# Attention output turned by a stored copy and turning transfers instead of on TensorE, with x's third piece in two and k's first part issued later

## The chip, the cores and the metric

The kernel runs on one core of a Trainium2 chip. The metric is device time in microseconds (us) for one execution, as the median of several runs. A core has five engines that run side by side and meet through semaphores: TensorE (PE; its weight loads are listed apart as PEld), VectorE (DVE), ScalarE (ACT), GpSimd (POOL) and SyncE (SP). SP computes nothing here; it issues transfers, and its instructions are taken strictly in order, as are those of every engine.

## The reference

Two branches on the same x (= A_q, 2048 tokens by 640 channels, bf16) are mixed by a gate per token.

```python
x = A_q
g = _sigmoid((x * gate_w).sum(-1, keepdims=True))
a = _A_ref(x, A_k, A_v, A_shift_k, A_ssm_k, A_ssm_D)
b = _B_ref(x, B_wqkv, B_wo)
return g * a + (1 - g) * b
```

Branch A takes a causal four-tap convolution of k per channel, multiplies it by v, convolves the product along the whole sequence with a kernel of 2048 taps per channel (by a transform of length 4096, plus `ssm_D` times the input) and multiplies by q. Branch B is attention with 32 heads of 20 channels, in which each token sees the 8 tokens at distances 0, 2, ..., 14 behind it, followed by the output projection:

```python
qkv = (x @ wqkv).reshape(B, S, 3, H, Dh)          # H = 32, Dh = 20
idx = pos[:, None] - off[None, :]                 # off = 0, 2, ..., 14
logits = jnp.einsum("bhsd,bhswd->bhsw", q, kg) * scale
attn = _softmax(jnp.where(mask, logits, -1e9), axis=-1)
o = jnp.einsum("bhsw,bhswd->bhsd", attn, vg)
return o.reshape(B, S, D) @ wo
```

## The kernel before

**Layout.** Even and odd tokens are two separate sequences ("parities") of 1024, since the attention's distances are even. Each is cut into 9 blocks of 114 queries that see 121 keys (`BQ`, `BK`), 18 blocks in all; the last block of a parity has 112 queries. x is wanted with channels on partitions (`xT`, five tiles of 128 channels): it is turned on its way in by turning transfers (`load_x`, line 291), for parity 0 in pieces of 256, 256 and 512 rows (`x00`, `x01`, `x02`), for parity 1 in two of 512 (`x10`, `x12`).

**Order.** Every step is a generator that yields one request per instruction group. Which generator goes next, and whether ScalarE or VectorE empties a PSUM buffer, was settled beforehand: the string `ORDER` has one letter per request, `ENGINES` one letter per free choice of engine, and `Plan.run` (line 159) only replays them. Each engine therefore has a fixed list. The PSUM is four slots of two banks, handed out in turn in that same order, so an instruction on TensorE also waits for the evacuation that last used its slot. The costs in the requests play no part in the replay.

**The steps, in rough order of time.**

- `heads` (line 374): first loads and constants. On POOL's queue: the gate's weights, the taps (`wraw`), k's first part (rows 50 to 63 of each group of 64, four transfers, line 399), and then the mask rows of the second key and query buffers (`masks`, line 369: a copy for keys, one for queries).
- `vproj` (line 470): value projection, 9 units of two blocks for each half of the heads; a unit is ten matmuls, evacuated to `VW`.
- `qkproj` (line 512): q and k projection, five channel tiles, three units of ten matmuls for q and for k, evacuated to `stg`; `fragger` (line 546) moves the heads' rows from there to 32-row slots of the key and query buffers, by transfers on POOL's queue (`kb`, `qb`). Eight sets of four heads share three buffers.
- `conv` (line 445): the four-tap convolution, on VectorE, from the last rows down, 7 instructions on 11 rows each; it needs k's parts as they land.
- `score_gen` (line 583), `pv_gen` (line 608): for each head set ten groups of scores, exponentials on ScalarE, two groups of attention times values, and on VectorE the normalisation into `oS` (tokens of a block on partitions, 18 blocks by 640 channels).
- `transform` (line 682): the forward transform in two stages (`s1_unit`, 10 units; `s2_unit`, 11 units) for the kernel h and the input u, each in two halves of the channels: "h units" and "u units" below. Stage 1 of u reads `vin` as weights. h's taps come in 16 slices on SP's queue (line 333); POOL adds `ssm_D` to h (line 711) when its half is there; G (the second stage's matrix) comes in four pieces into the buffer that the convolution leaves.
- `swaps` (line 743): per half, eight transfers of 320 KB that write the transform of h with its partition halves exchanged (`Hw`). From the fourth on each is preceded by a `link` (line 277), a tiny transfer that waits for the one three before.
- `op_tr` (line 780): the attention output turned on TensorE, 18 matmuls against an identity for each of five channel tiles, each tile copied from PSUM to `oT` by one instruction. `oT` lies where h's taps lay.
- `products` (line 695): 22 products on VectorE per half; they need the half's `Hw` whole.
- `outproj` (line 796): 16 groups of 40 matmuls from `oT` and `wo`, evacuated with the factor 1 - g to `bl`.
- `inverse1` (line 763), `final` (line 847), `load_q`, `gate_q`, `stores`: the inverse transform in two stages, q gated by g, the mix, and the stores of the result.

The order in which the generators are numbered by `ORDER`'s letters is that of lines 885 to 890.

Of the kernel before, what the change touches and what calls it, by code (L numbers as in the profile page):

```python
# [17 lines left out]
S = 2048  # L18
D = 640
# [32 lines left out]
def _np_bf16(a):  # L52
    return np.asarray(a, dtype=np.float32).astype(ml_dtypes.bfloat16)
# [35 lines left out]
def attn_consts():  # L89
# [19 lines left out]
    return dict(mm=_np_bf16(mm.reshape(128, BK + BQ)), ident=_np_bf16(np.eye(128)))  # L109
# [4 lines left out]
aaaafawaxaaaaaaaxxwwwwaxwgaaxxjjwfwxwfffxxwfwjxxfjjxffffffffffjacjjjccjjcjaxffcwaawwjwacacccccxacfcwwawbjajffaajcjcbaddjdcdajdfbdddaajajddcc  # L114
djjccddajadcddedcbddbadcaccfxxxffcfecjfacedxbjaefcbbcddjdddjadjdfdjfcddcjddajcdddedaddacfjedjddfddadddjeccacccdadjcaddjdafcdaecdfdecddjcecdc
cdacdjdbaffjddaaacjfedjdddcaejffaadjddfdjdfddbdedjaadddbbejdefccchaacaacjcjckcccaaejbcmcchdkcdaddjachcdjdddjdddjdjddkdadhjekadddjaddikcaekja
ddmdjadjdlcAcccAdceddAedddAbAdAAddecdddcccdAdeccdcddAdAdcAeadcedAddAAdddcAaadAdAAdAdlednddddaeaadAaAadelddkedddlAdAdAAdAdAAAlddledldldAdemmB
ddBAABBABeeBBBlABoBCABBBBBBBABlCABClABqAqBkCACqAqAqACCDDCDCCCCCCClCCqlllCDqCDqlDCpDqCqqpBBBBBBBBBBBBDDDDBpBBBBBpBBBCBlDCCDCCCCDCDDDDDDCDClpC
CCCDpppppppDpDpyDyDplyyDrrryrDCyryDDyDpypryCDryCCrDyyyyCryCDrDDrCyCyDDDrDyDrDppyppprypppyprrrprpDslEsErEEsEsEEEEEEEEEzzzzzzzzzzzzzzzzzzzzzzE
EEEEsFsEFFtsFssEFssFFtFFtFtsFFFFFFFsFFssFrtsrtsusFusuuuuuuuuuuuuuuuuuuuuurrruruuuuuuusuuturururrrvutruuuuuvurvvruvvuvvvvvvvvvvvvvvvvvvvvvv  # L120
"""
ENGINES = """
ADDAADAAAAAAAAAAAAAADAADDDDAADADADDDDAADDAADDDDDDDDDDDDDADDDADDADAADADAADADADAADADAADADADADADADADADADAADADADADADADADAADADAAAAADAAAAAADAAAAAA
AAAAAAAAAAAAAADADDADADDDAAAADDDDAAADAASDASSSASSSSSSSSSSSSSSSSSSASASAS
# [53 lines left out]
def kernel(  # L178
# [21 lines left out]
    def raw(ap, off, dims):  # L200
        return bass.AP(tensor=ap.tensor, offset=ap.offset + off, ap=dims)
# [6 lines left out]

    p0 = ctx.enter_context(tc.tile_pool(name="p0", bufs=1))
# [7 lines left out]
    ident = p0.tile([128, 128], BF, name="ident")  # L217
# [151 lines left out]
    def masks(copier, e):  # L369
        nc.gpsimd.memset(ksets[e][:, KW:], 0.0)  # L370
        copier(ksets[e][:, 0:KW].rearrange("p (b k) -> p b k", k=BK), mm[:, 0:BK].unsqueeze(1).to_broadcast([128, NB, BK]))
        copier(qsets[e][:].rearrange("p (b k) -> p b k", k=BQ), mm[:, BK:BK + BQ].unsqueeze(1).to_broadcast([128, NB, BQ]))

    def heads():
# [22 lines left out]
        a, b = KR[0]  # L397
        for q in range(4):
            nc.gpsimd.dma_start(kin[32 * q:32 * q + 32, 3 + a:3 + b, :], raw(k2, a * D + CH[q], [[64 * D, 32], [D, b - a], [1, QC]]))
        masks(nc.gpsimd.tensor_copy, 1)  # L400
# [5 lines left out]
        for q in range(4):  # L406
            at(f"k{q}0", 15500.0)
# [3 lines left out]
    def late():  # L411
# [16 lines left out]
    XP = {"x00": (0, 0, 256), "x01": (0, 256, 512), "x02": (0, 512, 1024), "x10": (1, 0, 512), "x12": (1, 512, 1024)}  # L428
# [179 lines left out]
    def pv_gen():  # L608
        n = 0
        for t in range(NT):  # L610
            for gis, b0, na in PARTS:
# [21 lines left out]
                for a in range(na):  # L633
                    dst = oS[0:BQ, b0 + 6 * a:b0 + 6 * a + 6, 80 * t:80 * t + 80].rearrange("p b (h d) -> p b h d", h=4)
                    nc.vector.tensor_tensor(dst, Ov[:, a, :, 0:DH].rearrange("p (b h) d -> p b h d", h=4),
                                            rv[:, a].rearrange("p (b h) -> p b h", h=4).unsqueeze(3).to_broadcast([BQ, 6, 4, DH]), ALU.mult)
        mark("oS", r)
# [141 lines left out]

# [142 lines left out]
```

## Time and profile before

| | us |
|---|---|
| median of 3 runs | 232.32 |
| lowest, highest | 231.50, 232.58 |
| the profiled execution's own time | 232.02 |
| its span, first to last instruction | 229.9 |

| engine | busy, us | share of the span | instructions |
|---|---|---|---|
| TensorE, matmuls | 209.2 | 91% | 3802 |
| VectorE | 189.2 | 82% | 259 |
| ScalarE | 165.3 | 72% | 215 |
| POOL | 63.6 | 28% | 144 |

The mean clock granted to TensorE is 0.924 of full speed. 34.92 MB are moved in 74,742 packets, 58,276 of which are under 512 bytes.

How the lines below are read. The chain of waits gives, in order of time, start, length and what the chain was on: an engine with its line, or a transfer with its two tensors; "SPq" is SP issuing a transfer. A line of the timeline or of the group table reads: line of the kernel, engine, operation, output<-input by the program's names, shapes, count; the group table goes on with busy time, mean ns of one, and the idle time ahead of them with what ended it. Names such as `sc`, `pj`, `psv`, `s`, `i`, `op`, `tr` are PSUM tiles of the steps above. `SX` holds h's first half after the convolution, `Hs` the second, `UC` holds u.

### The profile page before, as it was taken

Reading aid. Unit: us, or ns where it says so; the run is one execution under the profiler, and the core shown is the slowest. Engines: PE = TensorE matmul, PEld = TensorE weight load, DVE = VectorE, ACT = ScalarE, POOL = GpSimd, SP = SyncE. Lnnn points to the kernel's source line nnn. Section 1 sums busy time; section 2 is a strip of 40 time slices with the busy share of each in tenths; the row PEclk is TensorE's granted clock in tenths of the full one; section 3 lists DMA queues with packets and bytes.
Section 4 is the critical chain, followed back from the end, with each engine's and each line's share of the span. In section 5 each row is a group of like instructions: output and inputs, shape, how many; then the busy total and the mean of one; then the engine's idle time right before and its main releaser. Section 6 shows DMA issues by size and latency. Waiting matters only on the chain.

```text
span 229.9 us, 8777 instructions
## 1 busy us (share of the span) xinstructions
PE 209.2 (91%) x3802; PEld 168.2 (73%) x3802; DVE 189.2 (82%) x259; ACT 165.3 (72%) x215; POOL 63.6 (28%) x144
## 2 busy tenths in 40 slices
PE   6859999999899999999898998999899999999940
PEld 2647978857656766566676788898798899998930
DVE  4353999779868989977997679999999998979990
ACT  2012535378498888587888879979999999788960
POOL 8891005945734754745500000000000000000000
PEclk9997999999999999999855557999999999999996
DMA  7999856869999999797797661096887955921872
GB/s 171 205 232 232 169 173 142 171 117 170 145 158 174 150 156 156 117 139 125 139 139 215 182 204 41 3 222 157 174 189 161 227 98 117 199 35 25 196 183 66
DMA packets 74742, 34.92 MB, mean 152 GB/s; under 512 B 58276, under 2 KB 71152, under 8 KB 74704
## 3 DMA queue, kind: packets, MB, share of 16 engines
q1 hardware_dynamic: 68896, 26.93, 61.3%
q0 software_dynamic: 4080, 6.41, 13.4%
q10 hardware_dynamic: 1728, 1.02, 1.7%
q8 instruction: 29, 0.48, 1.0%
q14 instruction: 9, 0.07, 0.1%
HBM read 18.43 MB, written 2.62 MB: 92 GB/s over the span
## 4 chain that ended last, share of the span: by engine, by line
PE 55%; DVE 18%; DMA 10%; POOL 5%; ACT 4%; issue 4%; SPq 2%; DVEq 0%; POOLq 0%; ACTq 0%
PE pj L527 13%; PE i L772 8%; PE psv L478 8%; PE op L810 6%; PE s L672 6%; PE sc L595 6%; DMA xT<-in_A_q_dram 5%; DVE Hs L207 4%; ACT ETall L602 4%; PE s L656 4%; PE O L623 4%; DMA kb<-stg 3%; DVE SX L873 3%; DVE SX L870 3%; DMA Dz<-in_A_ssm_D_dram 2%
## 5 line engine op out<-in xcount | busy, mean ns | idle before, releaser
L602 ACT ACTIVATE ETall<-sc 121x912 bf16<-121x912 f32 (+1 forms) x80 | 63.8, 858 | 10.5 <-PE sc L595 9.9
L527 PE MATMUL pj<-xT,Wqk 128*128 128x342 bf16 (+1 forms) x300 | 48.8, 312 | 0.3 <-DVE stg L207 0.3
L527 PEld LDWEIGHTS <-Wqk 128*128 128x128 bf16 x300 | 27.9, 98 | 15.0 <-issue 0.2
L205 ACT CAST UC<-s 128x960 bf16<-128x960 f32 (+2 forms) x32 | 29.4, 980 | 1.8 <-PE s L656 1.2
L478 PE MATMUL psv<-KX,xT 128*121 128x320 bf16 x180 | 27.1, 310 | 3.9 <-DMA xT<-in_A_q_dram 2.7
L478 PEld LDWEIGHTS <-xT 128*121 128x121 bf16 x180 | 24.8, 139 | 6.0 <-DMA xT<-in_A_q_dram 3.0
L572 POOL DMA_DIRECT2D qb<-stg x36 | 18.1, 505 | 35.6 <-ACT stg L205 21.8
L595 PE MATMUL sc<-qb,kb 31*128 31x114 bf16 x576 | 24.2, 232 | 2.3 <-ACT ETall L602 0.6
L436 DVE TENSOR_TENSOR KX<-KX 128x1760 bf16<-128x1760 bf16 (+1 forms) x24 | 24.6, 1042 | 0.4
L810 PE MATMUL op<-wo,oT 128*32 128x320 bf16 x640 | 24.0, 303 | 0.3 <-ACT SX L866 0.3
L205 ACT CAST VW<-psv 121x640 bf16<-121x640 f32 x13 | 8.9, 696 | 20.9 <-PE psv L478 20.9
L595 PEld LDWEIGHTS <-kb 31*128 31x128 bf16 x576 | 14.4, 101 | 12.3 <-issue 8.9
L672 PEld LDWEIGHTS <-SX 64*128 64x128 bf16 x512 | 20.5, 100 | 3.5 <-issue 2.8
L810 PEld LDWEIGHTS <-oT 128*32 128x32 bf16 x640 | 21.2, 140 | 1.4 <-issue 0.2
L205 ACT CAST stg<-pj 128x684 bf16<-128x684 f32 (+1 forms) x14 | 10.4, 742 | 16.4 <-PE pj L527 10.0
L572 POOL DMA_DIRECT2D kb<-stg x36 | 18.1, 507 | 11.6 <-DVE stg L207 5.6
L207 DVE CAST stg<-pj 128x726 bf16<-128x726 f32 (+1 forms) x16 | 14.3, 896 | 7.9 <-PE pj L527 4.7
L207 DVE CAST SX<-s 128x1024 bf16<-128x1024 f32 (+1 forms) x15 | 17.7, 1195 | 2.9 <-PE s L672 2.0
L443 DVE TENSOR_TENSOR KX<-KX 128x1760 bf16<-128x1760 bf16 (+1 forms) x18 | 18.8, 1043 | 0.4
L623 PEld LDWEIGHTS <-ETall 121*128 121x128 bf16 x576 | 16.4, 98 | 2.3 <-issue 1.2
L772 PE MATMUL i<-F,Hw 128*128 128x128 bf16 x160 | 18.0, 219 | 0.0
L772 PEld LDWEIGHTS <-Hw 128*128 128x128 bf16 x160 | 17.9, 114 | 0.0
(76 smaller groups left out, 350.7 us busy)
## 6 DMA issues: line engine op xcount, KB each, us to landing
vin<-in_A_v_dram SPq DMA_DIRECT2D x8, 320.0 KB
h_lin<-in_A_ssm_k_dram SPq DMA_DIRECT2D x16, 160.0 KB
Hw<-SX SPq DMA_DIRECT2D x8, 320.0 KB
Hw<-Hs SPq DMA_DIRECT2D x8, 320.0 KB
SX<-in_A_q_dram SPq DMA_DIRECT2D x16, 160.0 KB
kb<-stg POOLq DMA_DIRECT2D x28, 85.1 KB, 4.2
qb<-stg POOLq DMA_DIRECT2D x28, 80.2 KB, 4.3
SX<-cf_G SPq DMA_DIRECT2D x4, 512.0 KB
```

The costliest lines, as they stand in the source:

```text
L205: nc.scalar.copy(dst, src)
L207: nc.vector.tensor_copy(dst, src)
L436: eng.tensor_tensor(d, kin[:, n + 3 - j:n + 3 - j + m, :], w.to_broadcast([128, m, QC]), ALU.mult)
L478: nc.tensor.matmul(ps[0:BK, i, 0:320], lhsT=xT[:, dt, s0:s0 + BK], rhs=Wv[:, dt, 320 * hf:320 * hf + 320], start=(dt == 0), stop=(dt == ND ...
L527: nc.tensor.matmul(ps[:, i, 0:n], lhsT=Wqk[:, dt, w, 128 * ft:128 * ft + 128], rhs=xT[:, dt, s0:s0 + n], start=(dt == 0), stop=(dt == NDT ...
L572: nc.gpsimd.dma_start(dst[r0:r0 + rows, 0:wd], stg[fa - f0:fb - f0, 0:wd])
L595: nc.tensor.matmul(sc[:, hh, BQ * bb:BQ * bb + BQ], lhsT=kb[r:r + DH + NF, BK * b:BK * b + 128], rhs=qb[r:r + DH + NF, BQ * b:BQ * b + BQ] ...
L602: nc.scalar.activation(ETall[0:BK, e, :, 0:BQ * nb], sc[0:BK, :, 0:BQ * nb], ACT.Exp, scale=SCALE)
L623: nc.tensor.matmul(O[:, (b - b0) // 6, c0:c0 + 21], lhsT=ETall[0:BK, e, hh, BQ * bb:BQ * bb + 128], rhs=VW[0:BK, b, 4 * t + h4, :], start= ...
L672: nc.tensor.matmul(ps[:, c, 160 * jj:160 * jj + 160], lhsT=st["G"][rows, j0 + jj, rr, :], rhs=Am[rows, rr].rearrange("p o (q j) l -> p j ( ...
L772: nc.tensor.matmul(d, lhsT=st[(key, P)][:, c, o + il // 4, :, il % 4], rhs=M[:, k, :], start=(k == 0), stop=(k == 1), skip_group_check=True)
L810: nc.tensor.matmul(op[c:c + 32, tt, 0:320], lhsT=oT[:, ft, h, 32 * e:32 * e + 32, a], rhs=wo[:, ft, 320 * w:320 * w + 320], start=(ft == 0 ...
```

## The change

The turning on TensorE goes. In its place a generator `keep_o` stores the attention output to a DRAM buffer `o_d` (two parities, 1024 tokens, 640 channels) in three parts of the channels, as the head sets are done (sets 0 to 3, 4 and 5, 6 and 7): four transfers per part on SP's queue, two for the first 112 rows of all blocks and two for the last two rows of the first eight blocks. `op_tr` then reads it back by four turning transfers of 512 tokens each, also on SP's queue, into an `oT` with another order of its columns; the output projection takes its weights from there at a step of 32 columns. The identity and its load go. x's third piece becomes two of 256 rows (`x02`, `x03`). k's first part is issued behind the key mask's copy on POOL instead of ahead of it. `ORDER` and `ENGINES` are new strings.

```diff
-    return dict(mm=_np_bf16(mm.reshape(128, BK + BQ)), ident=_np_bf16(np.eye(128)))
+    return dict(mm=_np_bf16(mm.reshape(128, BK + BQ)))
...
     def loads():
-        yield from load_x("x00", 0, 0, 256, 1400.0, 4550.0)
-        yield from load_x("x01", 0, 256, 256, 2800.0, 3400.0)
-        yield from load_x("x02", 0, 512, 512, 4300.0, 3100.0)
+        yield from load_x("x00", 0, 0, 256, 1400.0, 5100.0)
+        yield from load_x("x01", 0, 256, 256, 2800.0, 2700.0)
+        yield from load_x("x02", 0, 512, 256, 2800.0, 2300.0)
+        yield from load_x("x03", 0, 768, 256, 2800.0, 1900.0)
...
-    def masks(copier, e):
+    def masks(copier, e, between=()):
         nc.gpsimd.memset(ksets[e][:, KW:], 0.0)
         copier(ksets[e][:, 0:KW].rearrange("p (b k) -> p b k", k=BK), mm[:, 0:BK].unsqueeze(1).to_broadcast([128, NB, BK]))
+        for f in between:
+            f()
         copier(qsets[e][:].rearrange("p (b k) -> p b k", k=BQ), mm[:, BK:BK + BQ].unsqueeze(1).to_broadcast([128, NB, BQ]))
+
+    def k_first():
+        a, b = KR[0]
+        for q in range(4):
+            nc.gpsimd.dma_start(kin[32 * q:32 * q + 32, 3 + a:3 + b, :], raw(k2, a * D + CH[q], [[64 * D, 32], [D, b - a], [1, QC]]))
...
-        a, b = KR[0]
-        for q in range(4):
-            nc.gpsimd.dma_start(kin[32 * q:32 * q + 32, 3 + a:3 + b, :], raw(k2, a * D + CH[q], [[64 * D, 32], [D, b - a], [1, QC]]))
-        masks(nc.gpsimd.tensor_copy, 1)
+        masks(nc.gpsimd.tensor_copy, 1, (k_first,))
...
-        g = yield Req("G", 560.0, move=200.0)
-        nc.gpsimd.dma_start(ident[:], ca["ident"].ap())
-        mark("ident", g)
...
+            mark(f"oS{t}", r)
...
+    o_d = dpool.tile([2, HS, D], BF, name="o_d")
+
+    def keep_o():
+        rest = HS - BQ * (NBP - 1)
+        for part, (t0, t1) in enumerate(((0, 4), (4, 6), (6, 8))):
+            a, b = 4 * DH * t0, 4 * DH * t1
+            for par in range(2):
+                r = yield Req("S", 520.0, [ev(f"oS{t1 - 1}")], move=2600.0 * (t1 - t0) / 4 + 500.0)
+                nc.sync.dma_start(raw(o_d[:], par * HS * D + a, [[D, rest], [BQ * D, NBP], [1, b - a]]), oS[0:rest, NBP * par:NBP * par + NBP, a:b])
+            for par in range(2):
+                r = yield Req("S", 520.0, move=100.0)
+                nc.sync.dma_start(raw(o_d[:], (par * HS + rest) * D + a, [[D, BQ - rest], [BQ * D, NBP - 1], [1, b - a]]), oS[rest:BQ, NBP * par:NBP * par + NBP - 1, a:b])
+            mark(f"kept{part}", r)
+
     def op_tr():
-        yield Req("Z", 0.0, [ev("oS"), ev("hs10"), ev("hs11"), ev("ident")])
-        oT = p0.tile([128, NDT, 2, 64, 16], BF, name="oT", tag="HL")
+        yield Req("Z", 0.0, [ev("kept2"), ev("hs10"), ev("hs11")])
+        oT = p0.tile([128, NDT, 2, HS], BF, name="oT", tag="HL")
         st["oT"] = oT
-        for ft in range(NDT):
-            g = yield Req("P", 18 * 53.0, [ev("oS")], take=1, mode="f", mm=18)
-            tr = psum(g, "tr", (128, 2, HS), BF)
-            for b in range(NB):
-                par, j = b // NBP, b % NBP
-                w = min(BQ, HS - BQ * j)
-                nc.tensor.transpose(tr[:, par, BQ * j:BQ * j + w], oS[0:w, b, 128 * ft:128 * ft + 128], ident[0:w, 0:w])
-            r = yield Req("AD", dict(A=175.0 + 0.834 * 2048, D=140.0 + 0.54 * 2048), [g.done], give=g.banks)
-            copy(r.eng, oT[:, ft].rearrange("p h m a -> p m h a"), tr[:].rearrange("p r (n h a) -> p (r n) h a", h=2, a=16))
-            mark(f"oT{ft}", r)
+        for n in range(4):
+            par, i = n // 2, 512 * (n % 2)
+            g = yield Req("S", 4400.0, [ev("kept2")] if not n else [], move=2900.0)
+            nc.sync.dma_start_transpose(oT[:, :, par, i:i + 512], o_d[par, i:i + 512, :])
+            mark(f"oT{n}", g)
         mark("oTall", g)
...
-            g = yield Req("P", 40 * 38.0 + 60.0, [ev(f"oT{ft}") for ft in range(NDT)], take=1, mode="g", mm=40)
+            g = yield Req("P", 40 * 38.0 + 60.0, [ev(f"oT{n}") for n in range(4)], take=1, mode="g", mm=40)
...
-                            nc.tensor.matmul(op[c:c + 32, tt, 0:320], lhsT=oT[:, ft, h, 32 * e:32 * e + 32, a], rhs=wo[:, ft, 320 * w:320 * w + 320],
+                            nc.tensor.matmul(op[c:c + 32, tt, 0:320], lhsT=oT[:, ft, e].rearrange("p (n k) -> p k n", k=32)[:, t + tt], rhs=wo[:, ft, 320 * w:320 * w + 320],
```

What the new order moves, read off the two strings request by request. TensorE: the last three value units of the second half (blocks 12 to 17) go from the first two head sets to the fifth, one of them from ahead of the first scores; the second unit of the third q tile comes ahead of the second set's scores; the last k tile's last unit comes three score groups later; two units of h's second half that ran ahead of the last attention-value group run behind it; stage 2 of u's first half is finished ahead of the output projection. SP: the first two parts of the stored copy stand among the last slices of h, the pieces of G and `wo`; the third part stands ahead of the first swap; the turning transfers stand behind the third, sixth, seventh and eighth swap of the first half; all pieces of T (the last stage's matrix) come behind the last swap. VectorE: evacuation of value unit 3 (second half) behind the first three taps of the convolution; 26 evacuations between the last normalisation and the first product.

More of the change, by code (lines that the diff above doesn't have):

```diff
@@ L116 @@
[L116 to L119, printed above, removed]
@@ L885 @@
     for gen in (loads, late, fragger, score_gen, pv_gen, conv, bulk, conv_v, conv_end, qkproj, gate, load_GT, h_slot, p2_slot,
-                u_slot, swaps, op_tr, outproj, load_q, gate_q, final, stores):
+                u_slot, swaps, keep_o, op_tr, outproj, load_q, gate_q, final, stores):
         plan.add(gen())
```

22 lines of the change are left out of this document (13 added, 9 removed).

## The prediction

> **What bounds the kernel now.** I read the page's busy shares first, then the chain of waits in order of time, then a table by stretch, then SP's transfer queue.
>
> ```profile
> PE 209.2 (91%) x3802; PEld 168.2 (73%) x3802; DVE 189.2 (82%) x259; ACT 165.3 (72%) x215; POOL 63.6 (28%) x144
> PE 55%; DVE 18%; DMA 10%; POOL 5%; ACT 4%; issue 4%; SPq 2%; DVEq 0%; POOLq 0%; ACTq 0%
> ```
>
> TensorE is busy nearly throughout and carries 55% of the chain. In order of time (start, length, what):
>
> ```profile
> 0.75 1.39 SPq L293
> ...
> 4.86 11.47 DMA xT<-in_A_q_dram
> 16.37 4.38 PE psv L478 x20
> ...
> 29.22 1.45 PE pj L527 x10
> ...
> 42.12 2.72 PE psv L478 x20
> ...
> 47.74 0.33 PE sc L595 x15
> ...
> 62.16 0.38 PE sc L595 x7
> ...
> 138.67 0.66 DVE oS L635
> ...
> 153.56 0.79 PE s L656 x16
> 154.35 1.03 PE tr L790 x18
> ...
> 166.15 2.85 PE s L672 x72
> 169.00 2.88 PE op L810 x79
> ...
> 187.42 17.99 PE i L772 x320
> ```
>
> Five marks follow: the wait for x's third piece up to 16.33; the second head set's scores at 62.16; the end of the last attention normalisation at 139.33 (call it T0); the first output-projection matmul at 169.0; the end of the inverse step's matmuls at 205.4. From there to the end of the span (229.9) are 24.5 us. The stretches that matter (columns: PE, PEld, DVE, ACT, POOL busy; granted clock; DMA share; GB/s):
>
> ```profile
> 17.80:21.00 3.20, 3.20 (x14) 2.49 (x13) 0.22 (x1) 0.69 (x1) 0.56 (x1) 0.50 1.07 257
> 112.00:139.30 27.30, 26.01 (x536) 20.30 (x535) 21.67 (x27) 22.52 (x29) 1.20 (x5) 0.52 0.77 183
> 139.30:169.00 29.70, 27.83 (x606) 24.87 (x606) 29.30 (x31) 28.16 (x32) 0.00 (x0) 0.98 0.54 123
> ```
>
> From T0 to 169 VectorE and ScalarE are full (29.30 and 28.16 of 29.70), TensorE nearly so, and DMA is half idle. That is where the turning on TensorE sits now, and where the change puts transfers.
>
> **Removed: the turning on TensorE.** The row of 1.03 us above is one of five groups of 18 turning matmuls, some 5.3 us together; the copies behind them are
>
> ```profile
> L207 DVE COPY oT<-tr 128x2048 bf16<-128x2048 bf16 x5 | 6.1, 1223 | 0.3 <-issue 0.2
> ```
>
> Both leave the full stretch after T0. But the written order gives VectorE 26 evacuations between T0 and its first product, where it had 20, five copies and the gate, so its road to the first product stays at 29 to 30 us. Two h units (stage 1, second half) also move behind T0. The identity's load on POOL goes, one issue of some 0.6 us that nobody waited for.
>
> **The start.** With the third piece in two, the value projections of blocks 4 and 5 start when 256 rows are there. The idle on TensorE ahead of 16.37 goes, and with it the half clock behind it (the row of 17.80): 20 matmuls took 4.38 there, and 2.72 at 42.12, so 1.66. With the idle of 2.72 (13.65 to 16.37) that is 4.4. Against it stands k's first part:
>
> ```profile
> 8.03 5.62 PE L478 MATMUL psv<-KX,xT 128*121 128x320 bf16 x40 [0.87 <-PE wu L387]
> 6.57 1.91 POOL L399 DMA_DIRECT2D KX<-in_A_k_dram  x3
> 8.78 0.73 DVE L371 COPY kb<-mm 128x2178 bf16<-128x2178 bf16 x1 [1.88 <-DMA mm<-ca_mm]
> 10.44 2.00 POOL L371 COPY kb<-mm 128x2178 bf16<-128x2178 bf16 x1
> 21.53 2.05 DVE L436 TENSOR_TENSOR KX<-KX 128x1760 bf16<-128x1760 bf16 x2
> KX<-in_A_k_dram POOLq DMA_DIRECT2D x4, 140.0 KB, 7.3
> ```
>
> Its four issues now stand behind POOL's mask copy, which can begin at 8.78 and takes 2.00; at 0.64 each they end at 13.3; with 7.3 to landing that is 20.6. VectorE's order has three taps (1.03 each) ahead of the copy of value unit 3, second half, itself as long as a tap: done at 24.7. The second q projection unit takes that copy's PSUM slot, and TensorE reaches it at 13.65 + five value units of 1.36 + one projection of 1.45 = 21.9. So TensorE waits 0 (k landing within 4.5) to 2.8. I take the middle, 1.4, for a start **3.0 earlier**; bounds 0 (a wait of 2.8 that halves the clock once more) and 4.4.
>
> **Attention.** One value unit (1.36) leaves the work ahead of the first scores: they start 4.4 earlier, at 43.4. The second set's scores hang on POOL's fragments, whose order behind the first set's last scores is unchanged, so they too come 4.4 earlier, at 57.8. From there to T0 TensorE does three value units more (+4.1), one projection unit less (-1.6) and two h units less (the row below and its like, -1.5). Three scores, an attention-value group and two h units of the second kind now run ahead of the stretch at half clock (the row of 112.00), which I put at -0.8 (bounds 0 and -2).
>
> ```profile
> 135.53 0.79 PE s L656 x8
> ```
>
> T0 = 139.33 - 4.4 + 4.1 - 1.6 - 1.5 - 0.8 = 135.1: **-4.2**.
>
> **The stored copy and the turning transfers.** Twelve stores join SP's queue. The last four wait for T0; behind them stand swaps, which could not start before T0 + 3.4 anyway (two h units of 0.8 each behind the last normalisation's PSUM slot, a cast of 1.0, the rest signalling), so that wait holds nothing up. From there SP's queue is the path:
>
> ```profile
> 0.75 9.82 SPq L293 DMA_TRANSPOSE xT<-in_A_q_dram  x3
> 11.26 5.87 SPq L293 DMA_TRANSPOSE xT<-in_A_q_dram  x1
> 19.89 4.75 SPq L293 DMA_TRANSPOSE xT<-in_A_q_dram  x1
> 148.27 2.37 SPq L758 DMA_DIRECT2D Hw<-SX  x3
> 163.18 0.56 SPq L279 DMA_DIRECT2D mm<-Hw  x1
> 163.78 0.51 SPq L758 DMA_DIRECT2D Hw<-SX  x1
> 166.10 3.64 SPq L758 DMA_DIRECT2D Hw<-Hs  x3
> 178.89 0.46 SPq L758 DMA_DIRECT2D Hw<-Hs  x1
> ```
>
> A turning transfer of 512 rows holds SP for 4.75 to 5.87; 256 rows held it 1.39 on an empty queue (the chain's first row), which bounds 512 from below at 2.8. I take 4.75, the row nearest in traffic. Ahead of the fourth one's end stand three swaps (2.37), four turns (19.0) and five swaps with their links (1.07 each, 5.4): T0 + 30.2. For the landing, x's third piece shows 5.8 from the end of its issue (10.57) to 16.33, on a full queue; here DMA has room, so I take 3.5, between that and 1.5 (a drained queue: three quarters of the last turn already moved while it was issued). The first output matmul starts at T0 + 33.7 = 168.8. The evacuations would allow about T0 + 30.5, so 3.2 us are TensorE waiting: 33.7 in place of 29.7, **+4.0**. The weights' wider step (64 B a column) I put at nothing: the u units load 128 columns at a step of 160 B and ran 16 matmuls in 0.79.
>
> **Behind it.** Four forward units (2.85 / 6 each) have moved ahead of the output projection: **-1.9**, and the inverse's matmuls end at 168.8 + 36.4 - 1.9 = 203.3. Do the products keep up?
>
> ```profile
> 182.24 0.66 DVE L700 TENSOR_TENSOR Hs<-UC,Hs 128x960 bf16<-128x960 bf16 x1
> 194.03 0.48 DVE L700 TENSOR_TENSOR Hw<-UC,Hw 128x640 bf16<-128x640 bf16 x1
> ```
>
> The second half's swaps took 16.1 at most (three at 166.10, the last issued at 178.89, the first product on them at 182.24); from T0 + 30.2 = 165.3 that is 181.4. The products on them took 12.3, to 193.7; half of 17.99 behind them ends at 202.7, within 203.3. At the very end VectorE gets two output groups and gives one gating group of four to ScalarE:
>
> ```profile
> L817 DVE TENSOR_TENSOR bl<-op,omg 128x640 bf16<-128x640 f32 x3 | 2.5, 822 | 0.5 <-PE op L810 0.5
> L844 DVE TENSOR_SCALAR SX<-SX,g_nat 128x320 bf16<-128x320 bf16 x28 | 6.4, 295 | 0.0
> ```
>
> That is 2 x 0.82 less 4 x 0.24 (they overlap by some 0.06 each): **+0.7**.
>
> **Sum**: -4.2 + 4.0 - 1.9 + 0.7 = -1.4. The profiled execution took 232.02 around its span of 229.9, so 230.6; the median of the three runs lies 0.3 above it. I forecast **230.8**, between the two, with a range of its own of 228.5 to 233.
>
> **Rivals.**
>
> *The turns run faster.* At 2.8 a piece the path is 7.8 shorter and the evacuations decide: T0 + 30.5, 3.2 less, 227.6. For it: a DMA share of only 0.54 after T0. Against: no piece of 512 rows was below 4.75. The Trainium skill, "DMA: Bandwidth & Descriptors", section "Latency and other measured facts", gives a turning transfer 261 GB/s, an estimated 2.5 us for 655 KB; the trace's rows are half as fast. Chance 0.12.
>
> *The turns run slower, and the kernel with them.* Between swaps a piece may cost 5.87: 4.5 more on TensorE's wait and on the second half's swaps alike, and a wait of 7.7 halves the clock again (1.66): 237.0. From 5.1 a piece on (1.4 / 4 more) the gain is gone. For it: 5.87 was paid beside other loads, and swaps are other loads. Against: those loads filled DMA (share 1.07 at 17.80), swaps do not. Chance 0.24. The Trainium skill, "TensorE: Matmul & The Clock Gate", section "HAM oscillation", puts the idle that lowers the clock at over about 3.4 us; here 2.7 was enough. By the rule my forecast's wait of 3.2 is free of it, by the row it could add 1.66.
>
> *The start gives nothing* (k late, clock halved again): 3.0 lost, 233.8. Chance 0.11.
>
> *The stored copies crowd out h.* SP's order now has two large stores (645 KB each) and two pieces of G (524 KB each) ahead of the last h slice:
>
> ```profile
> 124.52 0.56 POOL L711 TENSOR_TENSOR h_lin<-h_lin,Dz 128x80 bf16<-128x80 bf16 x1 [11.84 <-DMA SX<-cf_G]
> 100.00:110.00 10.00, 9.80 (x198) 6.74 (x198) 8.01 (x11) 8.48 (x12) 5.22 (x11) 1.00 0.90 118
> ```
>
> 2.34 MB at 183 GB/s (row of 112.00) are 12.8 us: the add on h comes at 124.5 + 12.8 - 4.2 = 133.1, and the h units want it at about 137. At 118 GB/s it is 140.1, 3.1 late: 233.9. Chance 0.07.
>
> **Numbers.** Forecast 0.46: 0.33 faster by over 0.5% (1.16 us, about what a measurement of this kernel can tell from no change), 0.09 within, 0.04 slower. Faster turns 0.12, all faster. Slower turns 0.24: 0.23 slower, 0.01 within. The last two 0.18: 0.13 slower, 0.05 within. Together 0.45, 0.15, 0.40. The range takes in both prices of the turn: 226.5 to 237.
>
> **What would show it.** In the new profile: no half clock near 18 us; first scores near 43.4; T0 near 135; four turning transfers of 4.75 us on SP's queue between T0 + 5 and T0 + 30; TensorE idle some 3 us ahead of the first output matmul near 168.8. I am wrong if T0 is not earlier by 2 at least, if a turn holds SP above 5.1, or if VectorE stands idle ahead of the second half's products beyond 182.

## The result, and the profile after

The changed kernel took 240.07 us (median of 4 runs, 239.15 to 241.09) against 231.91 for the kernel before on the same chip: a ratio of 1.036, interval 1.029 to 1.044. It is **slower by 8 us**, and above the range of the prediction. The profiled execution took 241.09 around a span of 239.0, with a granted clock (the share of full speed that TensorE's clock was given) of 0.918. Runs of a kernel that took over 1.5% more than its fastest run, one or two in some kernels below, are left out of medians and ratios.

Shares of busy time and of the chain of waits, from the page of the changed kernel:

```profile
PE 206.2 (86%) x3712; PEld 163.1 (68%) x3712; DVE 188.7 (79%) x254; ACT 162.8 (68%) x215; POOL 63.7 (27%) x143
PE 34%; DVE 25%; DMA 20%; ACT 6%; issue 5%; POOL 4%; SPq 2%; ACTq 0%; DVEq 0%; POOLq 0%
```

TensorE was busy for 3 us less than before, in a span 9.1 longer: its share of the chain fell from 55% to 34%, and DMA's doubled (10% to 20%). The added time is waiting. The chain of waits in order of time (start, length, what) shows the first of it:

```profile
8.69 0.74 DVE kb L373
9.43 2.42 DVE qb L376
11.88 1.44 POOL KX L381 x3
13.32 9.04 DMA KX<-in_A_k_dram
22.54 2.07 DVE KX L439 x2
24.63 1.07 DVE KX L446
25.71 0.75 DVE VW L208
26.50 2.95 PE pj L530 x10
...
62.92 0.41 PE sc L598 x15
63.34 2.87 PE pj L530 x10
```

k's first part is issued behind POOL's key mask copy, lands at 22.4, and VectorE runs three taps before it empties value unit 3, whose PSUM slot the second q projection unit waits for. That unit then ran at half clock (2.95 for ten matmuls that take 1.45). TensorE's timeline at both ends of this wait, the first scores, and the two places behind the last normalisation (in brackets the idle time in front and what ended it):

```profile
9.77 9.27 PE L481 MATMUL psv<-KX,xT 128*121 128x320 bf16 x67
...
22.63 0.89 PE L481 MATMUL psv<-KX,xT 128*121 128x320 bf16 x5 [1.47 <-DMA xT<-in_A_q_dram]
26.50 2.95 PE L530 MATMUL pj<-xT,Wqk 128*128 128x342 bf16 x10 [2.98 <-DVE VW L208]
...
47.82 0.38 PE L598 MATMUL sc<-qb,kb 31*128 31x114 bf16 x8
...
173.60 0.35 PE L822 MATMUL op<-wo,oT 128*32 128x320 bf16 x2
176.79 2.84 PE L822 MATMUL op<-wo,oT 128*32 128x320 bf16 x38 [2.83 <-DMA oT<-o_d]
```

The wait for x's third piece is gone, as forecast: 67 matmuls run through in 9.27. But two new waits follow, 1.47 for x10 and 2.98 for the slot, and the first scores come at 47.82, where they were before (47.68), though one value unit less stands ahead of them. VectorE's timeline gives the last normalisation (it ends at T0 = 143.16) and the wait for the second half's swaps:

```profile
142.50 0.66 DVE L638 TENSOR_TENSOR oS<-O,rd 114x480 bf16<-114x480 f32 x1
...
191.92 0.66 DVE L704 TENSOR_TENSOR Hs<-UC,Hs 128x960 bf16<-128x960 bf16 x1 [6.68 <-DMA Hw<-Hs]
```

and SP's queue the four turning transfers and the swaps behind them:

```profile
150.54 3.09 SPq L805 DMA_TRANSPOSE oT<-o_d  x1
...
158.79 3.29 SPq L805 DMA_TRANSPOSE oT<-o_d  x1
...
163.70 4.16 SPq L805 DMA_TRANSPOSE oT<-o_d  x1
...
169.18 3.75 SPq L805 DMA_TRANSPOSE oT<-o_d  x1
173.06 3.82 SPq L762 DMA_DIRECT2D Hw<-Hs  x3
176.98 0.62 SPq L280 DMA_DIRECT2D mm<-wo  x1
180.05 0.59 SPq L280 DMA_DIRECT2D mm<-Hw  x1
...
188.50 0.51 SPq L762 DMA_DIRECT2D Hw<-Hs  x1
```

The chain shows what the last half of the inverse's matmuls waits for, the end of the products on VectorE at 204.20:

```profile
203.71 0.49 DVE Hw L704
...
204.25 9.07 PE i L776 x159
```

The span grew by 9.1: 3.8 up to T0 (139.33 to 143.16), 4.1 from there to the end of the inverse's matmuls (66.1 to 70.1, with rounding), and 1.2 at the end (24.5 to 25.7).

### The profile page after: what moved, and what is told of

Read it like the earlier page. It is cut to its first block, busy times and chain, and to the rows that moved or that the text cites. A ratio compares the mean times of both kernels' runs of the same rounds, so it can differ in the third digit from the quotient of the medians.

```text
span 239.0 us, 8618 instructions
## 1 busy us (share of the span) xinstructions
PE 206.2 (86%) x3712; PEld 163.1 (68%) x3712; DVE 188.7 (79%) x254; ACT 162.8 (68%) x215; POOL 63.7 (27%) x143
## 4 chain that ended last, share of the span: by engine, by line
PE 34%; DVE 25%; DMA 20%; ACT 6%; issue 5%; POOL 4%; SPq 2%; ACTq 0%; DVEq 0%; POOLq 0%
PE pj L530 10%; PE sc L598 5%; PE s L676 5%; DVE UC L208 4%; PE i L776 4%; DMA KX<-in_A_k_dram 4%; PE O L626 4%; DMA kb<-stg 4%; PE psv L481 4%; DMA mm<-Hw 3%; ACT ETall L605 3%; DMA mm<-ca_mm 3%; DVE Hs L208 3%; DVE Hw L704 3%; DVE SX L882 3%
## 5 line engine op out<-in xcount | busy, mean ns | idle before, releaser
L530 PE MATMUL pj<-xT,Wqk 128*128 128x342 bf16 (+1 forms) x300 | 51.2, 322 | 3.6 <-DVE VW L208 3.0
L530 PEld LDWEIGHTS <-Wqk 128*128 128x128 bf16 x300 | 28.8, 100 | 19.3 <-issue 3.5
L481 PE MATMUL psv<-KX,xT 128*121 128x320 bf16 x180 | 26.1, 301 | 3.1 <-issue 1.6
L822 PE MATMUL op<-wo,oT 128*32 128x320 bf16 x640 | 25.7, 313 | 3.1 <-DMA oT<-o_d 2.8
L598 PE MATMUL sc<-qb,kb 31*128 31x114 bf16 x576 | 22.5, 233 | 6.1 <-DMA kb<-stg 2.1
L481 PEld LDWEIGHTS <-xT 128*121 128x121 bf16 x180 | 23.9, 135 | 5.1 <-issue 2.5
L206 ACT CAST VW<-psv 121x640 bf16<-121x640 f32 x15 | 10.0, 697 | 23.9 <-PE psv L481 23.8
L676 PEld LDWEIGHTS <-SX 64*128 64x128 bf16 x512 | 21.8, 103 | 5.5 <-issue 4.8
L206 ACT CAST UC<-s 128x960 bf16<-128x960 f32 (+2 forms) x26 | 23.7, 986 | 0.7 <-PE s L676 0.3
L208 DVE CAST UC<-s 128x1024 bf16<-128x1024 f32 (+1 forms) x16 | 18.1, 1189 | 0.1
## 6 DMA issues: line engine op xcount, KB each, us to landing
qb<-stg POOLq DMA_DIRECT2D x28, 80.2 KB, 4.6
```

Of the source, the lines that this page charges most:

```text
L206: nc.scalar.copy(dst, src)
L208: nc.vector.tensor_copy(dst, src)
L481: nc.tensor.matmul(ps[0:BK, i, 0:320], lhsT=xT[:, dt, s0:s0 + BK], rhs=Wv[:, dt, 320 * hf:320 * hf + 320], start=(dt == 0), stop=(dt == ND ...
L530: nc.tensor.matmul(ps[:, i, 0:n], lhsT=Wqk[:, dt, w, 128 * ft:128 * ft + 128], rhs=xT[:, dt, s0:s0 + n], start=(dt == 0), stop=(dt == NDT ...
L598: nc.tensor.matmul(sc[:, hh, BQ * bb:BQ * bb + BQ], lhsT=kb[r:r + DH + NF, BK * b:BK * b + 128], rhs=qb[r:r + DH + NF, BQ * b:BQ * b + BQ] ...
L676: nc.tensor.matmul(ps[:, c, 160 * jj:160 * jj + 160], lhsT=st["G"][rows, j0 + jj, rr, :], rhs=Am[rows, rr].rearrange("p o (q j) l -> p j ( ...
```

## The experiments

Marks of all profiled executions, in us, read as above: the first scores, T0, when TensorE went on behind its last wait for the turned output, and what lies from T0 to the end of the span. "Ratio" is the time against the kernel before on the same chip. Each mark is of one execution. Four kernels do the same on their way to T0 but for the stores (after, plain for turning, link late, no turns): their first scores lie between 47.51 and 49.71, their T0 between 143.16 and 144.43. Three do the same behind it (after, k early, x whole): 94.7 to 95.8. A difference smaller than these tells nothing.

| kernel | ratio (interval) | median | first scores | T0 | output goes on | T0 to end |
|---|---|---|---|---|---|---|
| before | 1 | 231.9 | 47.68 | 139.33 | T0 + 29.6 | 90.6 |
| after | 1.036 (1.029-1.044) | 240.07 | 47.82 | 143.16 | T0 + 33.6 | 95.8 |
| after, k early | 1.032 (1.027-1.037) | 238.72 | 42.63 | 140.73 | T0 + 32.9 | 95.3 |
| after, x whole | 1.043 (1.035-1.050) | 240.96 | 48.58 | 143.82 | T0 + 32.5 | 94.7 |
| after, plain for turning | 1.038 (1.029-1.047) | 239.96 | 47.51 | 143.86 | T0 + 32.8 | 94.0 |
| after, link late | 1.043 (1.037-1.048) | 241.16 | 49.71 | 144.43 | T0 + 33.0 | 94.7 |
| after, no turns | 1.018 (1.012-1.023) | 237.10 | 47.56 | 143.36 | T0 + 30.3 | 91.5 |
| k early, value units back | 1.015 (1.007-1.023) | 237.29 | 41.72 | 139.19 | T0 + 33.4 | 96.0 |
| before + x split | 0.983 (0.978-0.988) | 228.06 | 44.99 | 135.41 | T0 + 29.4 | 90.7 |
| before + k late | 0.990 (0.983-0.997) | 229.32 | 44.16 | 136.39 | T0 + 29.4 | 90.5 |
| before + both | 1.000 (0.996-1.003) | 231.47 | 46.28 | 138.58 | T0 + 29.4 | 90.3 |
| before + turns | 1.047 (1.040-1.055) | 243.38 | 46.15 | 137.97 | T0 + 38.2 | 102.0 |
| all edits, old order | two runs, no interval | 241.0 | 45.71 | 138.18 | T0 + 38.4 | 102.0 |
| old order to T0, new behind | 1.014 (1.011-1.017) | 235.74 | 44.27 | 136.10 | T0 + 33.8 | 97.7 |

**k's first part early.**

```diff
-        masks(nc.gpsimd.tensor_copy, 1, (k_first,))
+        k_first()
+        masks(nc.gpsimd.tensor_copy, 1)
```

> The changed kernel with k's first part issued ahead of POOL's key mask copy, as it was before the change; all else as changed. Theory 1 (k late): k's first part lands some 2.5 to 4 us sooner than 22.4, VectorE's three taps begin by 19, the wait of 2.98 us on TensorE for value unit 3's copy and the half clock in the projection behind it go, the first scores come 3 to 5 us before 47.8 and the run takes 235.5 to 238 us. Rival (x10's late landing or the order sets the start): the first scores stay within 1.5 us of 47.8 and the run within 1 us of 240.

The first scores came 5.2 us sooner, so the reading of the start holds. But T0 came only 2.4 sooner, and the time of 238.72 is above the expected 235.5 to 238; its ratio (1.032) is not clear of the changed kernel's (1.036). TensorE's timeline of this run, with a line of the chain of waits behind it:

```profile
44.40 0.38 PE L599 MATMUL sc<-qb,kb 31*128 31x114 bf16 x8 [1.39 <-ACT stg L206]
...
57.65 0.80 PE L599 MATMUL sc<-qb,kb 31*128 31x114 bf16 x16 [1.19 <-DMA kb<-stg]
...
84.72 0.41 PE L599 MATMUL sc<-qb,kb 31*128 31x114 bf16 x16 [1.79 <-DVE stg L208]
85.06 2.19 PE L531 MATMUL pj<-xT,Wqk 128*128 128x349 bf16 x10
```

```profile
58.45 2.65 PE pj L531 x10
```

These are waits inside attention, and behind them projections of 2.65 and 2.19 us that take 1.56 to 1.67 at full clock. The last of the three waits began on VectorE:

```profile
83.75 1.73 DVE L208 CAST stg<-pj 128x726 bf16<-128x726 f32 x2 [1.44 <-DMA qb<-stg]
```

It could not overwrite the staging buffer until the fragments of the projection two before had left it. So the second finding is that attention in the new order makes little of an earlier start: of 5.2 us, 2.8 are lost again by T0.

**x's third piece whole.**

```diff
-        yield from load_x("x02", 0, 512, 256, 2800.0, 2300.0)
-        yield from load_x("x03", 0, 768, 256, 2800.0, 1900.0)
+        yield from load_x("x02", 0, 512, 512, 4300.0, 3100.0)
+        yield Req("S", 0.0)
```

> The changed kernel with x's third piece in one transfer of 512 rows, as before the change; all else as changed. Theory 1 (the split gains TensorE's wait of 2.7 us and the half clock behind it, but k's late landing takes it back): with the piece whole TensorE idles again until 16.3 and the work behind arrives at the taps' wait later, so most of the loss overlaps: first scores 48 to 50.5, run 240 to 242.5. Rival (the split itself delays the second half's pieces x10 and x12, and that is what costs): first scores up to 2 us sooner than 47.8, run 237.5 to 239.5.

Within the first theory's numbers: behind the late k the split is worth nothing that marks or times can tell. The first scores came 0.8 later, which is less than they differ by themselves.

**Plain transfers for turning ones.** The attention output is not turned here.

```diff
-            nc.sync.dma_start_transpose(oT[:, :, par, i:i + 512], o_d[par, i:i + 512, :])
+            nc.sync.dma_start(oT[:, :, par, i:i + 512], raw(o_d[:], (par * HS + i) * D, [[4 * D, 128], [512, NDT], [1, 512]]))
```

> The changed kernel with the four turning transfers replaced by plain transfers of the same bytes from the same stored copy (the attention output is not turned, so what follows multiplies other numbers). Theory 2 (SP's queue, held by the turns, sets the output projection's start and the second half's swaps): the last of the four is issued about 12 us sooner, the evacuations decide instead, the first output matmul runs on at 173.6 without the later wait of 2.83, the swaps of the second half land 8 to 12 us before 191.9, and the run takes 234 to 237. Rival (VectorE's and ScalarE's evacuations set that stretch whatever the transfers take): 239 to 241.

The theory of SP's time fell. The fourth transfer was issued at 166.2, 6.7 us sooner than in the changed kernel, and TensorE waited just as long for it. SP's queue, TensorE's timeline, and the busy times by stretch (PE, PEld, DVE, ACT, POOL; granted clock; DMA share; GB/s):

```profile
165.58 0.61 SPq L805 DMA_DIRECT2D oT<-o_d  x1
```

```profile
176.62 2.89 PE L822 MATMUL op<-wo,oT 128*32 128x320 bf16 x38 [3.31 <-DMA oT<-o_d]
```

```profile
165.00:170.00 5.00, 4.85 (x123) 4.26 (x120) 4.98 (x6) 4.94 (x7) 0.00 (x0) 1.00 1.05 248
170.00:175.00 5.00, 3.13 (x74) 2.50 (x69) 4.37 (x7) 4.99 (x7) 0.00 (x0) 1.00 1.08 248
```

The piece took 10.4 us from the end of its issue to TensorE's going on, in a stretch where the DMA engines were full at 248 GB/s. So neither the turning nor SP's time makes the output late; what is left is the full DMA engines. The time fits the rival's 239 to 241, but not its reason, since TensorE waited for the transfer and not for evacuations. The second half's swaps, issued sooner, did gain: the first product on them came at 189.23, T0 + 45.4 for T0 + 48.8. That is less than the 8 to 12 us expected, and the rest gained at most 1.8. Here the inverse no longer waits for the products, but for TensorE's own road through the late output.

**The ordering transfer behind the last swaps.** In the order of requests (names for letters):

```diff
-  lnk(T0) lnk sw1.3 lnk sw1.4 lnk sw1.5 lnk sw1.6 lnk sw1.7 ... T0
+  lnk sw1.3 lnk sw1.4 lnk sw1.5 lnk sw1.6 lnk sw1.7 ... lnk(T0) T0
```

> The changed kernel with the 1-element transfer that orders the rotation matrix's load put behind all swaps instead of ahead of the last ones; all else as changed. Theory 3 (each ordering transfer writes the same element and waits until the one before has landed, so this one holds the last swaps 2.5 to 3 us): the second half's last swap is issued 2 to 3 us sooner than in the changed kernel, VectorE's wait of 6.7 us before it shrinks by as much, the products and the inverse end 2 to 3 us sooner, and the run takes 237 to 238.5. Rival (the matrix then comes too late, or the wait moves to the next ordering transfer): within 1 us of 240.

Half of what was expected. From the issue of the second half's first swap to the first product on them 17.5 us passed (173.53 to 191.00), against 18.5 to 19.1 in the five kernels with the new order behind T0, turning transfers and this transfer in its place. So it costs 1.0 to 1.6 us there, and not 2.5 to 3, for the wait moves in part to the next ordering transfer, which the rival had named; it is issued 2.8 us behind the third swap:

```profile
173.53 2.43 SPq L762 DMA_DIRECT2D Hw<-Hs  x3
178.77 0.63 SPq L280 DMA_DIRECT2D mm<-Hw  x1
```

At the end no gain is shown: the rest takes 94.7, as with x whole, and the time (241.16) lies above both expected ranges, with k landing later still in this execution and T0 1.3 later. The chain says why. The inverse's matmuls run through, without a wait for the products, behind the output projection, and end at T0 + 68.8, where those of x whole end at T0 + 69.0 behind the products:

```profile
195.24 17.99 PE i L776 x320
```

(The rotation matrix of the expectation is T, the last stage's matrix.)

**One edit each, in the old order.** x split alone (the inverse of the diff above), k late alone (the key mask copy ahead of k's four transfers), and both:

> The kernel before, in its own order, with x's third piece in two transfers of 256 rows and nothing else changed. Theory 1 (the split gives the start 4 to 5 us, as the run with k early showed: first scores at 42.6): first scores near 43.3, run 228 to 230, as far as the second set's scores follow. Theory 4 (the attention stretch gives the lead back: waits of 1 to 2 us for fragments and evacuations, each with a half clock behind it, take the time whenever it starts): first scores near 43.3, but the last normalisation within 1.5 us of 139.3, run 230.5 to 232. Rival (the split delays x10 and x12 and gains nothing): first scores within 1 us of 47.7.

> The kernel before, in its own order, with k's first part issued behind POOL's key mask copy, as the change has it, and nothing else changed. Theory 1 (k late delays VectorE's taps and with them value unit 3's copy): k's first part lands 2 to 3 us later, TensorE waits some 1.5 us for that copy behind its wait for x, first scores 48.5 to 51, run 232 to 235. Rival (x's third piece is later than k anyway): within 0.7 us of the kernel before.

> The kernel before, in its own order, with both the split of x's third piece and k's first part behind the key mask copy; no turning transfers, no stored copy. Theory 1: the lead of the split is lost at value unit 3's copy as in the changed kernel, first scores 47 to 48.5, run 231 to 233. Theory 5 (the order from the second set on, not the start, makes the changed kernel slow): the same here, since the order is the old one; the changed kernel's further 7 us are then not of the start. Rival (the start alone makes most of the loss): 235 or more.

Each alone **makes the kernel faster**, if by little: the split by 1.7%, the late k by 1.0%, with intervals below 1. Together they do nothing. The split's time is what theory 1 wanted. Its first scores came 2.7 sooner, not 4.4, and its lead reached T0 (135.41, 3.9 sooner). Both together took the 231.47 that theory 1 and theory 5 had in common, with first scores (46.28) sooner than the expected 47 to 48.5. That k's late issue gains was expected by none. TensorE's and VectorE's timelines of that run say why:

```profile
9.76 6.55 PE L480 MATMUL psv<-KX,xT 128*121 128x320 bf16 x47
```

```profile
21.15 2.06 DVE L438 TENSOR_TENSOR KX<-KX 128x1760 bf16<-128x1760 bf16 x2 [3.98 <-DMA KX<-in_A_k_dram]
```

With k's transfers out of the way, x's third piece lands whole before TensorE needs it: 47 matmuls run through where the kernel before waited 2.73. VectorE waits 3.98 for k, and in the old order nobody is behind it: value unit 3 is emptied ahead of the taps. With both edits the next piece of x is late instead:

```profile
23.60 3.61 PE L481 MATMUL psv<-KX,xT 128*121 128x320 bf16 x25 [2.77 <-DMA xT<-in_A_q_dram]
```

Either edit alone removes the wait for x's third piece (the split leaves 0.56 of it). Together they gain nothing more there, and TensorE waits 2.8 for x10, where with k late alone it waited 0.17. Why x10 is there only at 23.60, for 21.32 with k late alone, no run tells.

**The turn alone, in the old order.** Stores and turning transfers take the place of the turning on TensorE, at places in SP's queue like the changed kernel's:

> The kernel before with only the turning replaced: the stored copy and four turning transfers in SP's queue at places like the changed kernel's, the rest of the order as it was, x in four pieces, k early. Theory 2 (turns and their place in SP's queue cost what the changed kernel loses behind the last normalisation, 4.0 us, less the two evacuations it does not move): last normalisation near 139.3, first output matmul or its wait for the turned output ends at T0 + 33 to 34, run 234 to 237. Rival (the loss behind the last normalisation comes of the new order, not of the turns): 231 to 233.

Dearer than either expected:

```profile
176.21 4.24 PE L821 MATMUL op<-wo,oT 128*32 128x320 bf16 x60 [9.19 <-DMA oT<-o_d]
```

TensorE goes on at T0 + 38.2, 8.6 later than before, and the rest takes 102.0 for 90.6. Without other work moved ahead of the output projection, the turned output is 9 us late.

**No stores and no turns.** POOL writes zeros in their place, so the output lacks the attention part.

```diff
-                nc.sync.dma_start(raw(o_d[:], ...), oS[...])
+                pass
...
-            nc.sync.dma_start_transpose(oT[:, :, par, i:i + 512], o_d[par, i:i + 512, :])
+            nc.gpsimd.memset(oT[:, :, par, i:i + 512], 0.0)
```

> The changed kernel without the twelve stores and without the four turning transfers; POOL writes zeros into the turned tile instead, so the output lacks the attention part. Theory 2b (the transfers' bytes on DMA behind the last normalisation, not SP's time alone, make the output projection and the second half's swaps late): last normalisation within 1 us of 143.2, first output matmul without a later wait, the rest behind the last normalisation 89 to 91.5 us against 95.8, run 234 to 236.5. Rival A (the stores also slow the loads of h and the fragments, and with them attention): last normalisation 140 to 142 besides, run 231 to 233.5. Rival B (the evacuations and the order set the stretch): the rest stays at 94 us or more, run 238.5 or more.

T0 stays at 143.36, and the rest falls by 4.3, to 91.5, the edge of what theory 2b expected (the time, 237.10, is 0.6 above it). So the stores do not hurt attention by anything that shows; the transfers cost 4.3 us behind it. The second half's first swap is issued at T0 + 25.3, for T0 + 29.9. Of VectorE's wait ahead of the second half's products, 2.44 stay of 6.68:

```profile
187.82 0.66 DVE L704 TENSOR_TENSOR Hs<-UC,Hs 128x960 bf16<-128x960 bf16 x1 [2.44 <-DMA Hw<-Hs]
```

The busy times from T0 to TensorE's going on, first of the changed kernel, then without the transfers, over the same stretch:

```profile
143.16:176.79 33.63, 26.97 (x591) 23.33 (x585) 32.42 (x33) 31.18 (x35) 0.00 (x0) 0.96 0.92 186
```

```profile
143.16:176.79 33.63, 29.91 (x674) 26.05 (x674) 32.59 (x34) 32.37 (x38) 8.75 (x4) 0.97 0.50 110
```

DMA is at 0.92 of its time with them and at 0.50 without.

**The moved value units put back** (and k early). Requests, with the evacuations' engines as before the change:

```diff
   sc0.4.1 exp0.4.1
+  vp1.6 VW1.6 vp1.7 VW1.7 vp1.8
   ... 
+  VW1.8
   stg2q0
...
-  gate vp1.6 pj4q0 ... vp1.7 sc4.1.0 ... vp1.8 sc4.3.0
+  gate pj4q0 ... sc4.1.0 ... sc4.3.0
```

> The changed kernel with k's first part issued early (as in the run k early, 238.7) and the second half's last three value units put back behind the first set's last scores, where two of them stood before the change. Theory 5a (those units, moved into set 4 where TensorE has no slack, are what makes the stretch from the second set's scores to the last normalisation 82.8 us in the run with k early, against 77.2 before): second set's scores at 58 to 60, last normalisation at 136 to 138, run 234.5 to 236.5. Rival 5b (the stretch is long for the waits and half clocks of the new order's scores and projections wherever the value units stand): last normalisation 139.5 to 142, run 237.5 to 240.

In between: T0 came 1.5 sooner than with k early alone, of the 2.7 to 4.7 that theory 5a wanted, little more than T0 differs by itself (1.3), and the runs spread from 234.6 to 237.8. The units explain a part at most, not the stretch: from first scores to T0 it is still 97.5 us, where the old order takes 90.4 to 92.5.

**All edits in the old order**, and **the old order up to T0 with the new one behind it** (x split, k early, turns):

> All three edits (x's third piece in two, k's first part behind the key mask copy, stored copy and turning transfers) in the order of the kernel before. Theory 5 (the new order costs 4 to 5 us up to the last normalisation and gives 6 back behind it, by moving work ahead of the output projection that the turns delay): last normalisation 137.5 to 139, the rest 101 to 103 as in the run of the turn alone, run 240.5 to 243. Rival (the edits do not add up: the late k's transfers and the turns fall into different stretches and the order gains nothing): 238 or less, or last normalisation above 141.

> The old order up to the last normalisation, the new order for all that is left behind it; x's third piece in two, k's first part issued early, stored copy and turning transfers as in the change. Theory 5 (the new order before the last normalisation costs 4 to 6 us beside what k's late issue costs, the turns with the new order behind it some 4 to 5): last normalisation 134.5 to 136.5 as in the run with x split alone (135.4), the rest 94 to 96, run 231 to 234. Rival (the two halves of the order only work together, or the turns' transfers delay attention wherever it starts early): last normalisation 138 or more, or the rest 98 or more; run 236 or more.

Both as theory 5 expected, but for the hybrid's rest (97.7 where 94 to 96 was expected) and with it its time (235.74 for 231 to 234). Against all edits in the old order, the new order costs 5.0 up to T0 (143.16 for 138.18) and gives 6.2 back behind it (95.8 for 102.0). Against the run with k early, the old order alone brings T0 from 140.73 to 136.10: 4.6 us. Since the rest is dearer by 5 to 7 with the turns even where the new order stands behind T0, the best of all kernels is one without them: **x split alone, 228.06 us, 1.7% below the kernel before**.

## Why the prediction was wrong

It forecast a span of 228.5 (229.9 - 1.4); 239.0 came, 10.5 more. Three steps carry that: T0 8.0, from there to the inverse's end 1.9 (70.1 for 68.2), the end 0.5 (+1.2 for +0.7). Two of the three signs of being wrong that it named came: T0 was not earlier, and VectorE stood idle ahead of the second half's products up to 191.92.

**The start** (first scores 4.4 sooner by the forecast, 0.1 later in fact). The gain of the split was there: with k early the first scores stand at 42.63, for the forecast 43.4. The step that failed is "TensorE waits 0 to 2.8, I take the middle". k landed at 22.4, not 20.6: the mask copy took 2.56 for 2.00, the four issues 2.94 (11.23 to 14.17) for 2.56, and from there to the landing 8.2 passed for 7.3. (The row of 7.3 counts from the start of an issue, and the sum added it to the end; counted as the row does, the last of the four took 9.0.) The wait came to 2.98, the projection behind it lost 1.5 to the half clock, and a wait of 1.47 for x10 had no term at all. These are 5.9 against a gain of 4.4: the start came out 1.5 below its stated bound of 0, and only the value unit that had left (1.36) kept the first scores where they were. So the rival "the start gives nothing" was the nearest, and still too mild: not 3.0 but 4.5 of the forecast was lost. The row for the mask copy was that of an emptier moment: the copy now ran beside VectorE's own (2.42 in the chain above, 0.70 before). Why the landing took longer, with x10 beside it in place of x's third piece, no run tells. At T0 k's late issue is worth 2.4, by the run with k early.

**Attention** (+0.2 forecast from the second set's scores to T0, +3.1 came: 80.2 us for 77.2). The failed step is the sum of moved units, each at its own duration. That sum was about right: TensorE is busy for 73.9 us of the stretch before and 74.6 after. What had no term is what the units covered. TensorE's time in the stretch, before, after and with k early (length; PE, PEld, DVE, ACT, POOL busy; granted clock; DMA share; GB/s):

```profile
62.16:139.33 77.17, 73.93 (x1379) 52.47 (x1381) 63.94 (x81) 63.93 (x82) 28.82 (x76) 0.83 0.88 157
62.92:143.16 80.24, 74.61 (x1379) 53.45 (x1381) 63.85 (x83) 64.32 (x83) 31.13 (x78) 0.84 0.98 168
57.95:140.73 82.78, 77.41 (x1379) 54.52 (x1381) 64.01 (x83) 64.42 (x84) 31.46 (x79) 0.79 0.92 163
```

It stands idle for 3.2 us before and 5.6 after: the new order gives new waits, for fragments, staging buffers and PSUM slots. With k early it stands idle for 5.4, no more, but runs at 0.79 of full speed for 0.84, and the stretch takes 82.8. That the order is the cause is shown by the hybrid (4.6) and by the two kernels with all edits (5.0). Which of its many moves is not settled: the value units make 1.5 of it at most, and the staging buffers were seen to hold one wait; a third such buffer was not tried. With 2.4 for k and 4.6 for the order, 1.0 of T0's 8.0 stays without a name, no more than T0 differs by itself.

**The turns** (T0 + 33.7 forecast, T0 + 33.6 came). Right in sum, but by luck: two errors cancel. A turn held SP 3.57 us on average, not 4.75, 4.7 less for four; but the issues between them waited, and the fourth's issue ended at T0 + 29.8 for 30.2. What was wrong is "here DMA has room": the share was 0.92 in that stretch, for 0.54 before, and with plain transfers that hardly hold SP the output was no sooner. For the output SP's queue was not the bound that I took it for; the DMA engines were full. The rivals of faster and slower turns were both beside the point. The half clock that the forecast's wait might bring came too: behind the wait of 2.83, 38 matmuls took 2.84 us, where 40 take 1.58 without the transfers.

**Behind it.** The second half's swaps landed at T0 + 48.8 for the forecast 46.3. They were issued on time (from T0 + 29.9, for 30.2); the term that failed is "16.1 at most" from the first issue to the landing, which took 18.9. The ordering transfer for T (the last stage's matrix), issued at 176.98 among them, had no term; it is 1.0 to 1.6 of this, by the run with it behind the swaps. The turns' bytes are not the reason, for without them it took 19.2. In the old order with the split, the late k or both, where VectorE waited for the swaps too, it took 16.9 to 17.0. What makes the rest is open. The products ended at T0 + 61.0 for 58.6, and the inverse waited: here "do the products keep up" got a yes by 0.6 us, which was too thin. TensorE's own road came out near the forecast: in the kernels with plain transfers and with the link late, where the inverse does not wait for the products, it ends at T0 + 68.4 and T0 + 68.8, for 68.2. The two roads are so near to each other that shortening one shows the other. The evacuations, too, came out as forecast: without the transfers the first output matmul runs at T0 + 30.3, by the sum T0 + 30.5.

**h behind the stores.** POOL's add on h came at 135.6, between that rival's 133.1 and 140.1, and at 133.3 without the stores. It cost nothing that shows: T0 is the same without them.

## What to carry to other kernels

Where several transfers queue for full DMA engines, moving one can make another late: ask which piece is wanted next, and price a pair of moves together, not each alone. When work is moved out of a stretch, look at what it covered there, buffer by buffer, before you book its duration as a gain. And before you put bytes into a stretch for the sake of an engine's time, add up the bytes that have to land there by the same moment, the new ones with the old: a half-idle DMA share is that of the kernel without the new bytes, and an average over the stretch. Where two roads end at nearly the same time, price both; one edit shortens one of them only.

## What the runs showed that was not expected

- VectorE and POOL hold each other up when both copy in on-chip memory: VectorE's copy of 128x2052 took 0.70 us in the kernel before, ahead of POOL's, and 2.50 in the changed kernel, beside POOL's; POOL's copy of 128x2178 took 2.00 and 2.56. The timelines, of VectorE before and after and of POOL after:

```profile
9.42 0.70 DVE L372 COPY qb<-mm 128x2052 bf16<-128x2052 bf16 x1
```

```profile
9.34 2.50 DVE L376 COPY qb<-mm 128x2052 bf16<-128x2052 bf16 x1
```

```profile
8.72 2.56 POOL L373 COPY kb<-mm 128x2178 bf16<-128x2178 bf16 x1 [1.98 <-DMA mm<-ca_mm]
```

  VectorE's copy ends at 11.84, some 0.56 behind POOL's at 11.28, nearly its own length. It took 2.50 in both old-order kernels with k late, too, and 0.82 with k early, where POOL's copy begins behind it. The Trainium skill, "SBUF — State Buffer", section "Who interferes with whom", describes a port pair that the two lock for a whole instruction in turn; the trace agrees.
- A wait does not always halve TensorE's clock. Behind a wait of 2.73 in the kernel before, 20 matmuls took 4.38 us for 2.72; behind one of 2.77 in the old order with the split and the late k, 25 took 3.61, which is the full pace (0.144 us each, at a granted clock of 1.00). And with k early a wait of 1.19 was followed by a projection of 2.65 for 1.56. The length of one wait does not decide it, and no run here tells what does. The Trainium skill, "TensorE: Matmul & The Clock Gate", section "HAM oscillation", has the clock fall behind an idle time of more than about 3.4 us; here it fell behind shorter ones.
- How long a turning transfer of 512 rows holds SP is no fixed cost: 3.09 to 4.16 us between swaps in the changed kernel, 3.42 and 6.97 at its start, and 4.75 to 5.87 at the start of the kernel before.
